# Sums in halves, scores of two chunks in a row, and a projection in one piece: a fused linear attention and MLP on one core

## The chip, the cores and the metric

The kernel runs on one core of one Trainium2 chip. The metric is the time of one execution in microseconds on the device; of several runs the median is given. Beside each time stands one profiled execution, whose span (first to last recorded instruction) is a little shorter than its own time. "The clock" is the granted TensorE clock, 1.00 being full speed.

Engines are called as in the profile: PE (matmuls), PEld (PE's weight loads), DVE, ACT, POOL, and SP, which issues most DMAs here.

## The reference: what is computed

Two parts follow each other, for 4 batches, 8 heads, 768 tokens and 64 elements a head:

```
state = gamma[h] * state + k[t]^T v[t]          # per batch and head, gamma = 1 - 2**(-5-h)
y[t]  = q[t] . state / sqrt(64)
x     = y, heads side by side                   # [4, 768, 512]
h     = (x^T U V)^T                             # U 768x32, V 32x768: over tokens
u     = x + h
out   = u + relu(u w1) w2                       # w1 512x2048, w2 2048x512
```

The kernel takes and gives float32 and computes the matmuls on bfloat16 operands.

## The kernel before

**A planner sets the order.** Nothing is issued when the code reaches it. Every step is given to a planner (class Plan, L65) by `add` with its cost by engine, the tiles it reads and writes, a due time and sometimes a hold (no earlier than). `run` (L116) then picks, again and again, the step with the earliest start, and of several the one that is due first; the steps of an engine are emitted in that order, and the tile framework adds the waits. So the costs, the due times and the planner's model of when a load lands (`load_cast`, L350, is one) and when an earlier result is ready (`ready`, L25) decide the order of all five engines' instruction queues. A change of the PE's array form between two steps is charged 0.093 us (`SWITCH`). Operations of POOL and DVE that are marked with a lock are not laid beside each other, and `behind` (L329) makes POOL's operation wait for the DVE operation in front of it where the planner has them within 3 us.

**Work.** The MLP of batch b carries the attention of batch b + 1 beside it, so that PE always has matmuls: startup with batch 0's attention, then MLP(0) beside attention(1), MLP(1) beside attention(2), MLP(2) beside attention(3), and MLP(3) alone (main loop, L1139 to L1169).

*Attention of batches 0 and 1* goes by pairs of heads, with PE transposes (`pair`, L480). *Attention of batches 2 and 3* goes by chunks of 128 tokens with all 8 heads (`loads_chunk` L653, `chunk` L662): three loads of 256 KB by SP; k cast by POOL or ACT, q and v scaled by the decay on POOL; k and q transposed by two DMAs on SP (L687, kT and qT, 4 and 4 buffers); the score (eight matmuls in 64x128 form, two of them side by side on the two halves of the rows, L692) into the PSUM tile RR[0], which is two banks (keys RR0, RR1); the mask product a = score x mask on DVE, 1024 elements (L700); the state's matmul into the PSUM tile Y and its eviction to ns; `mixes`, the matmuls with the earlier state and with a, into RR[1] (key RR2); and the eviction of that to x.

*The low rank part.* `proj` (L737) multiplies x by U into Y, 24 matmuls in 128x32 form, given to the planner as two steps (token blocks 0 to 3, 16 matmuls, then 4 and 5, 8 matmuls). `expand` (L753) multiplies by V into RR and adds x (L770, DVE, 512 elements per instruction): u, in the place of x. `turn_u` (L797, L798) transposes u by six DMAs on SP into uT, `turn_lo` (L774) does batch 1's low part on PE.

*The MLP* (`mlp`, L818) has 16 "lo" groups of four matmuls with 512 columns (tokens 0 to 511), then 8 "hi" groups with two times 256 columns; each group ends in a relu of 512 elements per partition (L836 ACT, or L838 DVE) into gT. The product with w2 then follows for r = 0, 1, 2 (two blocks of 128 tokens each), by seven products of 8 matmuls each of a Strassen-like scheme (`prod`, L930) into the PSUM tiles M0 to M2. They take as operands gT itself and sums of its quarters S1, S2, S4 and a difference left in gT, made on DVE (`sums`, L890, recorded at the helper's L302 as S and gT), as well as T1 to T4, sums over w2 (`w2_sums`, L1126, recorded as T and w2b). DVE evicts the products (L945, r5, r6 and halves of o), POOL prepares t12, t22 and t21 (L948, from ACT's copy s1 of the first product and from u), and the output is stored (L987).

`sums(part, m0, nm_, at)` gives four dependent DVE operations: S1 = A01 + A11, A01 = A00 - A01, S2 = S1 - A00, S4 = A10 - S2. Part 0 is tokens 0 to 511 (r = 0, 1), in four quarters of two m each, part 1 is the rest (r = 2), in two halves of four m each: 512 elements per instruction in all of them.

PSUM is full: RR0 to RR3, Y, M0 to M2 are its eight banks.

The lines that the profile puts operations to are often helpers': L305 is every matmul but the transposes (L309), L302 a two-operand operation on DVE or POOL, L297 a copy on ACT, L299 one on DVE or POOL, L342 a load on SP.

Of the kernel before, what the change touches and what calls it, by code (L numbers as in the profile page):

```python
# [18 lines left out]
class Step:  # L19
# [181 lines left out]
def kernel(  # L201
# [459 lines left out]

    def chunk(b, n, at):  # L662
        (kin, kk), (qin, qk), (vin, vk) = (gets.pop((nm, b, n)) for nm in "kqv")
        kd, kdk = new_kb()
# [21 lines left out]
        for src, dst, sk, dk in ((kd, kT, kdk, kTk), (qd, qT, qdk, qTk)):  # L686
# [13 lines left out]
        add({"D": cD(2 * DM)}, lambda e: nc.vector.tensor_tensor(  # L700
            a[:, :2 * DM].rearrange("p (n t) -> p n t", t=P),
            RR[0].rearrange("p i (n t) -> p (i n) t", t=P),
            mask[:, None, :].to_broadcast([P, H, P]), op=ALU.mult),
            ["RR0", "RR1", "mask"], zz(ak), at + 0.3)

# [7 lines left out]
        def mixes(e):  # L713
            if n:
                prev = ns[:, ds(4 * ((n - 1) % 5), 4)]
                for c in range(NC):
                    mm(RR[1][:, 0, ts(c, P)], qT[:, ts(c, P)], prev[:, c], start=(c == 0))
            for c in range(NC):
                for i in range(2):
                    h = 2 * c + i  # L720
                    mm(RR[1][:, 0, ts(h, D)], av[:, i, c], vd[:, ts(h, D)],
                       start=(n == 0 and h == 0))
# [9 lines left out]
        add({"PE": 0.24 + (0.23 if n else 0)}, mixes,  # L732
            [qTk, *nsk, *zz(ak), *zz(vdk)], ["RR2"], at + 1.9, F, slack=sl)
        evac(xs[b % 2][:, n], RR[1][:, 0], DM, ["RR2"], xk(b, [n], ALLC), at + 2.4)


    def proj(b, at):  # L737
        sl = 0.3

        def f(js):  # L740
            def g(e):
                for j in js:
                    for c in ALLC:
                        mm(Y[ds(RK * c, RK), :P], Ub[:, j], xs[b % 2][:, j, ts(c, P)],
                           start=(j == 0), stop=(j == NCK - 1))
            return g
        add({"PE": 0.25}, f(range(4)), xk(b, range(4), ALLC) + ["Ub"], ["Y"], at,
            ("cn", "cn"), slack=sl)
        add({"PE": 0.13}, f(range(4, 6)), xk(b, range(4, 6), ALLC) + ["Ub"], ["Y"],
            at + 0.1, ("cn", "cn"), slack=sl)  # L750
        evac(pcs, Y[:, :P], P, ["Y"], ["pcs"], at + 0.3)

    def expand(b, j0, nj, at):  # L753
        def f(e):
            for j in range(j0, j0 + nj):
                for c in ALLC:
                    mm(RR[c // 2][:, c % 2, ts(j - j0, P)], V4[ds(RK * c, RK), ts(j, P)],
                       pcs[ds(RK * c, RK)])
        keys = [f"RR{c}" for c in ALLC]
        add({"PE": 0.057 * nj + 0.02}, f, ["pcs", "V4"], keys, at, ("rn", "rn"),  # L760
            slack=0.2)
        x = xs[b % 2]
        for j in range(j0, j0 + nj, 2):
            for z in range(2):
                cc = (2 * z, 2 * z + 1)
                xj = x[:, ds(j, 2), ts(z, 256)].rearrange("p j (c f) -> p c j f", c=2)
                src = RR[z][:, :, ds((j - j0) * P, 256)].rearrange(
                    "p c (j f) -> p c j f", f=P)
                kk = xk(b, (j, j + 1), cc)
                add({"D": cD(512)}, lambda e, xj=xj, src=src: nc.vector.tensor_tensor(  # L770
                    xj, src, xj, op=ALU.add), [f"RR{c}" for c in cc] + kk,
                    kk + [("u", b % 2, i, z) for i in (j, j + 1)], at + 0.3)

# [40 lines left out]
    def next_m():  # L814
        mring[0] += 1
        return f"M{(mring[0] - 1) % 3}"

    def mlp(b, T, span, banks=()):  # L818
# [26 lines left out]
        for m in range(NM):  # L845
# [21 lines left out]
            relu(gT[:, m, :LO], bank, [bank], [("g", m, 0)], at + 0.9)  # L867
        yield
        for m in range(0, NM, 2):
# [13 lines left out]
            relu(gT[:, ds(m, 2), LO:], bank, [bank], [("g", m, 1), ("g", m + 1, 1)],  # L883
                 at + 0.9)
# [5 lines left out]
        def sums(part, m0, nm_, at):  # L890
# [3 lines left out]
            def A(z, w):  # L894
                return ge[:, z, w, ms, r]
            ek = [("g", 2 * m, part) for m in range(m0, m0 + nm_)]
            ok = [("g", 2 * m + 1, part) for m in range(m0, m0 + nm_)]

            def sk(n):
                return [(n, m, part) for m in range(m0, m0 + nm_)]  # L900
            for dst, a_, b_, op, rd, wr in (
                    (S1[:, ms, r], A(0, 1), A(1, 1), ALU.add, ek + ok, sk("S1")),
                    (A(0, 1), A(0, 0), A(0, 1), ALU.subtract, ek, ek),
                    (S2[:, ms, r], S1[:, ms, r], A(0, 0), ALU.subtract,
# [17 lines left out]
        for r in range(NB):  # L922
            part = 0 if r < 2 else 1
            ek = [("g", m, part) for m in range(0, NM, 2)]
            ok = [("g", m, part) for m in range(1, NM, 2)]

# [49 lines left out]
            at = prod(be, gl(0, 1), T3, ek + tk, False)  # L976
            dve(ob[:, HD:], be, tmp["r5"], ["r5"], [(obk, 1)], at)
# [148 lines left out]
    def w2_sums():  # L1126
        w2e = w2b.rearrange("p (m z) (h n) -> p z h m n", z=2, h=2)
        for j in range(4):
            ms = ds(2 * j, 2)
            B11, B21, B22, B12 = (w2e[:, 0, 0, ms], w2e[:, 1, 0, ms],  # L1130
                                  w2e[:, 1, 1, ms], w2e[:, 0, 1, ms])
            for dst, a_, b_ in ((T3[:, ms], B22, B12), (B12, B12, B11),
                                (T2[:, ms], B22, B12), (T4[:, ms], B21, T2[:, ms])):
                add({"D": 0.5}, lambda e, dst=dst, a_=a_, b_=b_:
                    both(e, dst, a_, b_, ALU.subtract), [("w2", j)], [("T", j)],
                    T[0] + 14 + j, lock="D")
# [76 lines left out]
```

## Time and profile before

| | us |
|---|---|
| median of 3 runs | 223.75 (223.63 to 224.15) |
| the profiled execution's own time | 224.59 |
| its span | 222.8 |
| PE busy in it | 211.8 |
| DVE, ACT, POOL busy | 143.9, 111.7, 87.0 |

How to read it: the profile's durations come from the one profiled execution, so a sum over them is held against 224.59, and its difference to the median is carried along. A group of instructions is given as: line, engine, operation, tile written <- tiles read, partitions x elements and type, count | busy time in all, mean ns of one | idle time of the engine ahead of them and what ended it. For a matmul the first pair of numbers is the form of the array that it uses. In a timeline several instructions of one group in a row are merged: the start of the first, the time from it to the end of the last, and the count; matmuls overlap in the pipeline, so the end of one lies behind the start of the next. The wait in brackets is the engine's idle time ahead of the instruction and whose result ended it.

### The profile page before, as it was taken

How to read it: one execution, taken by the hardware profiler on the slowest of the kernel's cores; microseconds unless marked ns; L12 is line 12 of the kernel's file. 1: busy time of each engine (PE TensorE's matmuls, PEld its weight loads, DVE VectorE, ACT ScalarE, POOL GpSimd, SP SyncE). 2: the span in 40 equal slices, each digit the busy share in tenths (PEclk: the TensorE clock that was granted, in tenths of full speed). 3: DMA queues.
4: the chain of work that ended last, by engine and by line, in shares of the span. 5: the costliest groups of instructions: out<-in, count | busy, mean ns of one | idle time of the engine just before them, and what ended most of it. 6: DMA issues, size and time to landing. Idle time of an engine off the chain costs nothing.

```text
span 222.8 us, 5876 instructions
## 1 busy us (share of the span) xinstructions
PE 211.8 (95%) x2391; PEld 152.4 (68%) x2405; DVE 143.9 (65%) x297; ACT 111.7 (50%) x214; POOL 87.0 (39%) x143
## 2 busy tenths in 40 slices
PE   7867999999999999999999999999999999999993
PEld 2556644488788885457887875458888854588882
DVE  4486717998897636798677856867858525345332
ACT  8856537679684335678621105686510036761000
POOL 4665900114768554311368453316134510003330
PEclk9999999999999999999999999999999999999998
DMA  5999999999599979897479989986105730000222
GB/s 167 301 291 224 157 195 206 233 289 297 140 222 212 154 205 182 218 170 142 96 158 190 222 195 202 195 187 123 26 0 143 181 106 3 0 0 3 94 97 94
DMA packets 85163, 35.22 MB, mean 158 GB/s; under 512 B 59920, under 2 KB 83216, under 8 KB 85136
## 3 DMA queue, kind: packets, MB, share of 16 engines
q1 hardware_dynamic: 78944, 25.93, 55.0%
q0 software_dynamic: 6192, 8.91, 19.3%
q8 instruction: 19, 0.31, 0.6%
q14 instruction: 8, 0.07, 0.1%
HBM read 27.75 MB, written 6.29 MB: 153 GB/s over the span
## 4 chain that ended last, share of the span: by engine, by line
PE 63%; DVE 16%; DMA 7%; POOL 5%; issue 4%; ACT 2%; SPq 1%; POOLq 0%; DVEq 0%
PE M L305 51%; PE RR L305 8%; DVE S L302 4%; DMA in<-in_v_dram 4%; DMA in<-in_k_dram 3%; PE Y L305 3%; DVE T L302 2%; POOL t L302 2%; DVE x L770 2%; ACT gT L836 1%; DVE gT L302 1%; SPq L342 1%; DVE o L945 1%; POOL out_dram L987 1%; DVE x L299 1%
## 5 line engine op out<-in xcount | busy, mean ns | idle before, releaser
L305 PE MATMUL M<-uT,w1b 128*128 128x256 bf16 (+1 forms) x489 | 85.7, 324 | 0.7 <-issue 0.3
L836 ACT ACTIVATE gT<-M 128x512 bf16<-128x512 f32 x88 | 51.9, 597 | 34.1 <-PE M L305 33.5
L305 PEld LDWEIGHTS <-w1b 128*128 128x128 bf16 x512 | 48.0, 98 | 29.6 <-issue 0.8
L305 PEld LDWEIGHTS <-gT 128*128 128x128 bf16 x409 | 39.3, 99 | 10.6 <-issue 3.7
L302 POOL TENSOR_TENSOR t<-s,x 128x256 f32<-128x256 f32 x36 | 23.1, 669 | 34.9 <-DVE S L302 21.8
L305 PEld LDWEIGHTS <-S 128*128 128x128 bf16 (+1 forms) x336 | 28.1, 97 | 4.4 <-issue 0.4
L305 PE MATMUL M<-w2b,gT 128*128 128x256 bf16 x192 | 26.7, 273 | 0.1
L305 PE MATMUL M<-w2b,S 128*128 128x256 bf16 x192 | 26.1, 273 | 0.3 <-DVE r L945 0.3
L305 PE MATMUL M<-T,gT 128*128 128x256 bf16 x192 | 25.1, 273 | 0.5 <-DVE r L945 0.4
L302 POOL TENSOR_TENSOR qb<-in,gqn 128x512 bf16<-128x512 f32 x12 | 12.5, 1044 | 27.9 <-DVE S L302 11.6
L302 DVE TENSOR_TENSOR S<-gT 128x512 bf16<-128x512 bf16 x24 | 11.6, 485 | 18.0 <-ACT gT L836 17.9
L945 DVE TENSOR_TENSOR r<-M,t 128x256 f32<-128x256 f32 x24 | 10.1, 421 | 12.6 <-POOL t L302 11.7
L297 ACT ACTIVATE s<-M 128x256 f32<-128x256 f32 x12 | 4.6, 385 | 26.7 <-PE M L305 26.7
L987 POOL DMA_DIRECT2D out_dram<-o x18 | 10.1, 563 | 19.3 <-DVE o L945 19.3
L770 DVE TENSOR_TENSOR x<-RR,x 128x512 bf16<-128x512 f32 x24 | 15.2, 683 | 2.1 <-PE RR L305 2.1
L297 ACT ACTIVATE kb<-in 128x512 bf16<-128x512 f32 (+1 forms) x18 | 10.0, 582 | 13.0 <-DMA in<-in_k_dram 12.9
L700 DVE TENSOR_TENSOR a<-RR,mask 128x1024 bf16<-128x1024 f32 x12 | 14.6, 1218 | 1.4 <-PE RR L305 1.2
L302 POOL TENSOR_TENSOR vb<-in,gkn 128x512 bf16<-128x512 f32 x12 | 12.5, 1045 | 6.8 <-DMA in<-in_v_dram 3.0
L945 DVE TENSOR_TENSOR o<-M,r 128x256 f32<-128x256 f32 x24 | 10.1, 423 | 6.4 <-PE M L305 6.1
L305 PE MATMUL M<-T,S 128*128 128x256 bf16 x96 | 12.6, 273 | 0.0
L297 ACT ACTIVATE ns<-Y 64x256 bf16<-64x256 f32 (+1 forms) x24 | 9.4, 392 | 5.4 <-PE Y L305 3.8
L302 DVE TENSOR_TENSOR gT<-gT 128x512 bf16<-128x512 bf16 x24 | 11.5, 481 | 0.6
(104 smaller groups left out, 258.4 us busy)
## 6 DMA issues: line engine op xcount, KB each, us to landing
out_dram<-o POOLq DMA_DIRECT2D x18, 256.0 KB, 3.5
in<-in_q_dram SPq DMA_DIRECT2D x8, 384.0 KB, 6.0
in<-in_k_dram SPq DMA_DIRECT2D x12, 256.0 KB, 5.0
in<-in_q_dram SPq DMA_DIRECT2D x12, 256.0 KB, 4.5
in<-in_v_dram SPq DMA_DIRECT2D x12, 256.0 KB, 4.7
in<-in_k_dram SPq DMA_DIRECT2D x7, 384.0 KB, 6.2
in<-in_v_dram SPq DMA_DIRECT2D x7, 384.0 KB, 6.3
w2b<-in_moe_w_ch_dram POOLq DMA_DIRECT2D x4, 512.0 KB, 15.2
```

The source lines that it names most:

```text
L297: nc.scalar.activation(dst, src, AF.Copy)
L299: (nc.vector if e == "D" else nc.gpsimd).tensor_copy(out=dst, in_=src)
L302: (nc.vector if e == "D" else nc.gpsimd).tensor_tensor(dst, a, b, op=op)
L305: nc.tensor.matmul(out_, lhsT, rhs, start=start, stop=stop, skip_group_check=True)
L342: nc.sync.dma_start(out=dst, in_=src)
L700: add({"D": cD(2 * DM)}, lambda e: nc.vector.tensor_tensor(a[:, :2 * DM].rearrange("p (n t) -> p n t", t=P), RR[0].rearrange("p i (n t) -> ...
L770: add({"D": cD(512)}, lambda e, xj=xj, src=src: nc.vector.tensor_tensor(xj, src, xj, op=ALU.add), [f"RR{c}" for c in cc] + kk, kk + [("u", ...
L836: nc.scalar.activation(dst, src, AF.Relu)
L945: add({"D": cD(HD)}, lambda e: nc.vector.tensor_tensor(dst, bankof(bank)[:, :HD], src, op=op), [bank] + rd, wr, at - 2)
L987: lambda e: (nc.sync if last else nc.gpsimd).dma_start(out=dst, in_=src), rd, [("out", b, at)], at,
```

## The change

1. `sums` for part 0 in two halves rather than four quarters, and for part 1 in one set of all eight m, issued inside r == 0 of the product loop behind POOL's t's (it also names "t21" as read, so that it is planned behind them). `w2_sums` in two rather than four. So each instruction has 1024 rather than 512 elements. New keys "h" let the difference left in gT be waited for on its own. The planner's cost of each is `cD(1024, 2)` rather than 0.5.
2. `chunks` gives the scores of two neighbouring chunks as one PE step, the even one into RR[0], the odd one into RR[1]; `mixes` of each goes into its own RR[z].
3. `proj` is one step of 24 matmuls.
4. In batches 2 and 3 the additions of `expand` are due 6 us later.
5. The planner's model: a DVE result is ready for DVE 0.03 us after its end; `load_cast` is charged less; the first loads of batch 0's pairs are given an order among themselves.

The tokens of q in pairs, of which the change's short description speaks, are in none of its lines. `PART1` is set and not used. The diff, cut to its core:

```diff
@@ ready
-            t = max(t, p.free if p.eng == e else p.end + Plan.LAG[p.eng] + s.slack)
+            t = max(t, p.free if p.eng == e != "D" else
+                    p.end + (0.03 if p.eng == e else Plan.LAG[p.eng] + s.slack))
@@ load_cast
-            dma=(nd, 0.009 + size / 27200 * 1.17, 0.9, 1.0), hold=hold)
+            dma=(nd, 0.0045 + size / 27200, 0.9, 1.0), hold=hold)
@@ load_pair
+        first = [] if b else ["in"]
-                 P * n, 512, [(key, i) for i in g], at + 0.01 * g[0], hold,
+                 P * n, 512, [(key, i) for i in g] + first, at + 0.01 * g[0], hold,
@@ chunk
+        z = n % 2
+        keys = [f"RR{2 * z}", f"RR{2 * z + 1}"]
-                    mm(RR[0][:, i, ts(c, P)], kT[r, ts(c, P)], qT[r, ts(c, P)])
-        add({"PE": 0.24}, score, [kTk, qTk], ["RR0", "RR1"], at, ("rw", "rw"),
-            slack=sl)
+                    mm(RR[z][:, i, ts(c, P)], kT[r, ts(c, P)], qT[r, ts(c, P)])
+        yield score, [kTk, qTk], keys
-            ["RR0", "RR1", "mask"], zz(ak), at + 0.3)
+            keys + ["mask"], zz(ak), at + 0.3 + z)
-            [qTk, *nsk, *zz(ak), *zz(vdk)], ["RR2"], at + 1.9, F, slack=sl)
-        evac(xs[b % 2][:, n], RR[1][:, 0], DM, ["RR2"], xk(b, [n], ALLC), at + 2.4)
+            [qTk, *nsk, *zz(ak), *zz(vdk)], keys[:1], at + 1.9, F, slack=sl)
+        evac(xs[b % 2][:, n], RR[z][:, 0], DM, keys[:1], xk(b, [n], ALLC), at + 2.4)
+    def chunks(b, n, at):
+        two = [chunk(b, n + z, at + DN * z) for z in range(2)]
+        told = [next(c) for c in two]
+        def scores(e):
+            for f, _, _ in told:
+                f(e)
+        add({"PE": 0.45}, scores, [k_ for t_ in told for k_ in t_[1]],
+            [k_ for t_ in told for k_ in t_[2]], at + DN, ("rw", "rw"), slack=0.4)
+        for c in two:
+            list(c)
@@ proj
-        add({"PE": 0.25}, f(range(4)), xk(b, range(4), ALLC) + ["Ub"], ["Y"], at,
+        add({"PE": 0.37}, f(ALLN), xk(b, ALLN, ALLC) + ["Ub"], ["Y"], at,
             ("cn", "cn"), slack=sl)
-        add({"PE": 0.13}, f(range(4, 6)), xk(b, range(4, 6), ALLC) + ["Ub"], ["Y"],
-            at + 0.1, ("cn", "cn"), slack=sl)
@@ expand
-                    kk + [("u", b % 2, i, z) for i in (j, j + 1)], at + 0.3)
+                    kk + [("u", b % 2, i, z) for i in (j, j + 1)],
+                    at + (6.3 if b > 1 else 0.3))
@@ sums
-                add({"D": 0.5}, lambda e, dst=dst, a_=a_, b_=b_, op=op:
+                add({"D": cD(nm_ * (256 if part == 0 else 128), 2)},
+                    lambda e, dst=dst, a_=a_, b_=b_, op=op:
-        for q4 in range(4):
-            sums(0, 2 * q4, 2, T + unit * (0.864 * 4 * (q4 + 1) + 1.0))
-        for q4 in range(2):
-            sums(1, 4 * q4, 4, T + unit * (13.8 + 0.872 * 4 * (q4 + 1) + 1.0))
+        for z in range(2):
+            sums(0, 4 * z, 4, T + unit * (0.864 * 8 * (z + 1) + 1.0))
@@ mlp, product loop, behind the three pool(...) of t12, t22, t21
+            if r == 0:
+                sums(1, 0, 8, at + 1)
@@ w2_sums
-        for j in range(4):
-            ms = ds(2 * j, 2)
+        for j in range(0, 4, 2):
+            ms = ds(2 * j, 4)
@@ main loop
-                chunk(b, n, base + 2 + 4.6 * n)
+                if n % 2:
+                    chunks(b, n - 1, base + 2 + 4.6 * (n - 1))
```

More of the change, by code (lines that the diff above doesn't have):

```diff
@@ L701, in chunk @@
             a[:, :2 * DM].rearrange("p (n t) -> p n t", t=P),
-            RR[0].rearrange("p i (n t) -> p (i n) t", t=P),
+            RR[z].rearrange("p i (n t) -> p (i n) t", t=P),
             mask[:, None, :].to_broadcast([P, H, P]), op=ALU.mult),
-            ["RR0", "RR1", "mask"], zz(ak), at + 0.3)
+            keys + ["mask"], zz(ak), at + 0.3 + z)
         def state(e):
@@ L716, in mixes @@
                 for c in range(NC):
-                    mm(RR[1][:, 0, ts(c, P)], qT[:, ts(c, P)], prev[:, c], start=(c == 0))
+                    mm(RR[z][:, 0, ts(c, P)], qT[:, ts(c, P)], prev[:, c], start=(c == 0))
             for c in range(NC):
@@ L720, in mixes @@
                     h = 2 * c + i
-                    mm(RR[1][:, 0, ts(h, D)], av[:, i, c], vd[:, ts(h, D)],
+                    mm(RR[z][:, 0, ts(h, D)], av[:, i, c], vd[:, ts(h, D)],
                        start=(n == 0 and h == 0))
@@ L816, in next_m @@
         return f"M{(mring[0] - 1) % 3}"
+    PART1, DN = 24.0, 2.0
     def mlp(b, T, span, banks=()):
@@ L866, in mlp @@
                         [bank], at + 0.4 * z, F)
-            relu(gT[:, m, :LO], bank, [bank], [("g", m, 0)], at + 0.9)
+            relu(gT[:, m, :LO], bank, [bank], [("g", m, 0), ("h", m, 0)], at + 0.9)
         yield
@@ L882, in mlp @@
                     [w1key(m)], [bank], at + 0.4 * z, F)
-            relu(gT[:, ds(m, 2), LO:], bank, [bank], [("g", m, 1), ("g", m + 1, 1)],
+            relu(gT[:, ds(m, 2), LO:], bank, [bank], [("g", m, 1), ("g", m + 1, 1), ("h", m, 1)],
                  at + 0.9)
@@ L896, in sums @@
             ek = [("g", 2 * m, part) for m in range(m0, m0 + nm_)]
+            hk = [("h", 2 * m, part) for m in range(m0, m0 + nm_)]
             ok = [("g", 2 * m + 1, part) for m in range(m0, m0 + nm_)]
@@ L901, in sums @@
             for dst, a_, b_, op, rd, wr in (
-                    (S1[:, ms, r], A(0, 1), A(1, 1), ALU.add, ek + ok, sk("S1")),
-                    (A(0, 1), A(0, 0), A(0, 1), ALU.subtract, ek, ek),
+                    (S1[:, ms, r], A(0, 1), A(1, 1), ALU.add,
+                     ek + hk + ok + ["t21"] * part, sk("S1")),
+                    (A(0, 1), A(0, 0), A(0, 1), ALU.subtract, ek, hk),
                     (S2[:, ms, r], S1[:, ms, r], A(0, 0), ALU.subtract,
@@ L924, in mlp @@
             ek = [("g", m, part) for m in range(0, NM, 2)]
+            hk = [("h", m, part) for m in range(0, NM, 2)]
             ok = [("g", m, part) for m in range(1, NM, 2)]
@@ L975, in mlp @@
             dve(tmp["r5"], de, tmp["t22"], ["t22"], ["r5"], at)
-            at = prod(be, gl(0, 1), T3, ek + tk, False)
+            at = prod(be, gl(0, 1), T3, hk + tk, False)
             dve(ob[:, HD:], be, tmp["r5"], ["r5"], [(obk, 1)], at)
@@ L1127, in w2_sums @@
         w2e = w2b.rearrange("p (m z) (h n) -> p z h m n", z=2, h=2)
-        for j in range(4):
-            ms = ds(2 * j, 2)
+        for j in range(0, 4, 2):
+            ms = ds(2 * j, 4)
+            wk, tk = [("w2", j), ("w2", j + 1)], [("T", j), ("T", j + 1)]
             B11, B21, B22, B12 = (w2e[:, 0, 0, ms], w2e[:, 1, 0, ms],
@@ L1133, in w2_sums @@
                                 (T2[:, ms], B22, B12), (T4[:, ms], B21, T2[:, ms])):
-                add({"D": 0.5}, lambda e, dst=dst, a_=a_, b_=b_:
-                    both(e, dst, a_, b_, ALU.subtract), [("w2", j)], [("T", j)],
+                add({"D": cD(1024, 2)}, lambda e, dst=dst, a_=a_, b_=b_:
+                    both(e, dst, a_, b_, ALU.subtract), wk, tk,
                     T[0] + 14 + j, lock="D")
```

## The prediction

> **What bounds the kernel now.** Read first the page (busy time per engine, the chain that ended last), then the same busy times by stage.
>
> ```profile
> span 222.8 us, 5876 instructions
> ...
> PE 211.8 (95%) x2391; PEld 152.4 (68%) x2405; DVE 143.9 (65%) x297; ACT 111.7 (50%) x214; POOL 87.0 (39%) x143
> ...
> PE 63%; DVE 16%; DMA 7%; POOL 5%; issue 4%; ACT 2%; SPq 1%; POOLq 0%; DVEq 0%
> ```
>
> ```profile
> 0.00:33.00 33.00, 27.22 (x423) 16.89 (x428) 18.19 (x47) 21.66 (x41) 18.93 (x42) 1.00 1.05 223
> 33.00:84.50 51.50, 50.70 (x698) 38.31 (x698) 39.57 (x79) 32.70 (x63) 22.27 (x40) 1.00 1.02 218
> 84.50:132.20 47.70, 47.22 (x503) 33.86 (x505) 35.60 (x68) 21.79 (x43) 21.84 (x28) 1.00 0.92 175
> 132.20:179.70 47.50, 47.21 (x480) 34.48 (x481) 32.78 (x62) 20.10 (x40) 17.11 (x23) 1.00 0.64 129
> 179.70:222.80 43.10, 39.42 (x297) 28.89 (x296) 17.74 (x44) 15.48 (x27) 6.86 (x11) 0.99 0.14 50
> ```
>
> The columns after the length are the busy times of PE, PEld, DVE, ACT and POOL, then the granted clock. The stages are startup, then the MLPs of batches 0, 1, 2 and 3, each but the last with the next batch's attention beside it. From 33.0 to 179.7 us PE idles 0.80, 0.48 and 0.29 us, at a full clock. DVE is the next engine, with 12 to 15 us to spare in every stage. So from 33 us on, time comes only from what PE itself executes, or from these few idle moments. The waits of PE from 33 us on, with total, times and longest:
>
> ```profile
> PE M L305 <- DVE r L945: 0.6, 3, 0.3
> PE RR L305 <- DVE uT L299: 0.2, 1, 0.2
> PE M L305 <- DVE o L945: 0.2, 1, 0.2
> PE M L305 <- issue: 0.2, 1, 0.2
> ```
>
> All of PE's waits together are 1.2 us. Matmul ends are modelled, so distances between starts are the better measure below; by them such a stall is up to twice what its row says, some 2.2 us in all.
>
> **The change, part by part.** The two instruction orders agree on all engines for the first 34 us, and PE issues 2405 matmuls in both: no form of matmul changes, only the order. The startup (33 us) and what follows the last matmul stay.
>
> *1. Pairs of scores, and the projection in one go.* A score runs in 64-row form and the projection in 32-column form, among 128x128 work. PE's timeline in MLP(1), start and duration:
>
> ```profile
> 106.00 1.91 PE L305 MATMUL M<-uT,w1b 128*128 128x256 bf16 x16
> 107.84 0.40 PE L305 MATMUL RR<-qT,kT 64*128 64x128 bf16 x8
> 108.17 0.61 PE L305 MATMUL M<-uT,w1b 128*128 128x256 bf16 x4
> 108.84 1.91 PE L305 MATMUL M<-uT,w1b 128*128 128x256 bf16 x16
> 110.59 0.39 PE L305 MATMUL RR<-ns,qT 128*128 128x128 bf16 x4
> 111.92 1.04 PE L305 MATMUL M<-w2b,gT 128*128 128x256 bf16 x8
> 112.89 0.40 PE L305 MATMUL RR<-qT,kT 64*128 64x128 bf16 x8
> 113.22 1.05 PE L305 MATMUL M<-T,S 128*128 128x256 bf16 x8
> 114.10 1.04 PE L305 MATMUL M<-w2b,S 128*128 128x256 bf16 x8
> ...
> 117.27 0.41 PE L305 MATMUL Y<-x,Ub 128*32 128x128 bf16 x16
> 117.61 1.05 PE L305 MATMUL M<-T,gT 128*128 128x256 bf16 x8
> 118.59 0.29 PE L305 MATMUL Y<-x,Ub 128*32 128x128 bf16 x8
> 118.82 1.05 PE L305 MATMUL M<-w2b,S 128*128 128x256 bf16 x8
> ```
>
> Take starts. Sixteen matmuls ahead of a score last 106.00 to 107.84 = 1.84, ahead of full-size work 108.84 to 110.59 = 1.75: entering the 64-row form costs 0.09. Eight matmuls say the same: 111.92 to 112.89 = 0.97 against 113.22 to 114.10 = 0.88. A score lasts 0.33 from its start to the next work (107.84 to 108.17). Two scores in a row enter and leave that form once in place of twice; the exit taken at the price of the entry (a choice: its row shows only the 0.33 with the matmuls in it), a pair saves 0.2. Six pairs (batches 2 and 3, six chunks each): 1.2 us. The projection's sixteen last 0.34 and its eight 0.23, that is 0.12 once and 0.11 per eight; all 24 in a row should last 0.45 in place of 0.57, and one entry goes (117.61 to 118.59 = 0.98 against 0.88, 0.10): 0.22 a batch, 0.4 for two. Together 12 + 4 changes of form at 0.10 each: **−1.6**. It can't be hidden, since PE is solid in 84.5 to 179.7; lower end 0, if all of it turned into waits; upper end 1.6.
>
> *2. What the pair costs.* Both scores now wait for both chunks' transposed q and k. Tightest is batch 2's pair of chunks 4 and 5. Chunk 5's q is scaled on POOL, transposed by a DMA, and landed 3.5 us after issue; its score stood at 112.89 above:
>
> ```profile
> 105.94 1.04 POOL L302 TENSOR_TENSOR qb<-in,gqn 128x512 bf16<-128x512 f32 x1 [4.45 <-DVE S L302]
> ```
>
> ```profile
> L687 SPq DMA_TRANSPOSE qT<-qb x1: 1190/1190/1190, 107.0 to 107.0; - x1
> ...
> DMA to landing us min/median/max: 3.5/3.5/3.5
> ```
>
> So it landed at 107.0 + 3.5 = 110.5. In the new order PE reaches the pair at about 109.5. POOL's 4.45 us of waiting is for sums. Their last eight of 0.43 become four of 0.69 (item 3): 0.6 sooner; and a mask product of 1.22, that now stands between them, moves with its pair and may or may not stand there: the landing comes between 108.7 and 109.9. Bounds: 0 and 110.5 − 109.5 = 1.0; I take **+0.2**, since the estimate of the landing lies just ahead of need. The other five pairs stand 3 us and more behind their landings in the order.
>
> *3. Sums of 1024 elements.* The DVE's groups, mean ns behind the busy time:
>
> ```profile
> L770 DVE TENSOR_TENSOR x<-RR,x 128x512 bf16<-128x512 f32 x24 | 15.2, 683 | 2.1 <-PE RR L305 2.1
> L700 DVE TENSOR_TENSOR a<-RR,mask 128x1024 bf16<-128x1024 f32 x12 | 14.6, 1218 | 1.4 <-PE RR L305 1.2
> ...
> L302 DVE TENSOR_TENSOR S<-S,gT 128x512 bf16<-128x512 bf16 x24 | 10.2, 427 | 0.0
> ```
>
> 512 elements more cost 1218 − 683 = 535 ns with a PSUM operand, so 683 holds some 0.15 of fixed cost; a bf16 sum of 427 holds 0.15 + 0.27, and 1024 elements cost some 0.15 + 0.54 = 0.69 in place of 0.85. Bounds: 0.85 (nothing saved) and, at the other form's rate, 1.22. Ninety-six sums of this kind and 16 on w2 become 48 and 8: 56 x 0.16 = 9 us less DVE. It lies beside PE, so it is worth only the waits that it ends: I take the 0.80 of 33 to 84.5 as gone (the `DVE r` waits, where DVE is at 77%): **−0.8**, bounds 0 and −0.8, and of the wait `DVE uT` at the start of MLP(1) (0.2 by its row, up to twice that), half: **−0.2**, since one of these evictions passes from ACT to DVE.
>
> The Trainium skill, VectorE: DVE Perf Modes, section The TRN2 errata, gives a VectorE operation between SBUF tiles 58 cycles of fixed cost, 0.06 us at its 0.96 GHz; by that, an estimate, the 56 operations save 3.4 us and not 9, which would leave perhaps half of the waits and give 223.0. The 0.15 of the rows above speaks for the larger saving; no row here has a 1024-element bf16 sum.
>
> *4. Part 1's sums behind POOL's t's of r = 0.* They no longer stand ahead of t12. In the last batch this was a stall:
>
> ```profile
> 204.40 1.03 PE L305 MATMUL M<-T,gT 128*128 128x256 bf16 x8 [0.18 <-DVE r L945]
> ```
>
> That goes, but four sums of 0.69 then stand among the evictions of the products, which PE wants every 0.87 us: 0.2 to 0.3 late once. Even, **0**, bounds ±0.3. In MLP(1) the next step's t12 waits for the fourth of these sums on DVE: r6 comes up to 0.45 late there, while the 0.2 to 0.35 of `DVE o` (behind a mask product that moves away) goes: **+0.1**, bounds −0.35 and +0.45.
>
> *5. The planner believes in earlier loads and in DVE readiness 0.03 us after the end.* That is what reorders ACT. In the order after, the casts of batch 1's first k and q and kT (kb0 ahead of the first hi relu of MLP(0)) pass in among the eight hi relus. ACT now, and the first k's issue:
>
> ```profile
> 45.02 0.60 ACT L836 ACTIVATE gT<-M 128x512 bf16<-128x512 f32 x1 [0.27 <-PE M L305]
> ...
> 49.88 0.93 ACT L297 ACTIVATE kb<-in 128x384 bf16<-128x384 f32 x2
> ```
>
> ```profile
> L342 SPq DMA_DIRECT2D in<-in_k_dram x1: 384/384/384, 40.4 to 40.4; - x1
> ...
> DMA to landing us min/median/max: 6.2/6.2/6.2
> ```
>
> The load lands at 40.4 + 6.2 = 46.6. ACT has finished a relu at 45.6 and then waits 1.0 for it, with all hi relus queued behind. Then ACT has 8 relus (0.5 to 0.6), four pairs of casts (0.93) and one kT (0.8): 4.2 + 3.7 + 0.8 = 8.7 us in a stage in which PE needs 7.0. Late by 1.0 + 1.7 = 2.7; PE has two further M banks, 2 x 0.87 = 1.7 ahead: a stall of **+1.0**, bounds 0 (the casts fall behind the relus' slack) and 2.7 (no bank ahead).
>
> *6. u's additions later (batches 2, 3).* They follow the product's evictions. The third pair of additions, and the transposes that read them:
>
> ```profile
> 125.05 1.28 DVE L770 TENSOR_TENSOR x<-RR,x 128x512 bf16<-128x512 f32 x2
> ```
>
> ```profile
> 123.29 8.21 SPq L798 DMA_TRANSPOSE uT<-x  x6
> ```
>
> Each transpose takes SP 8.21 / 6 = 1.37, so the third pair is read from 128.8, and was ready at 126.3: 2.5 us of cover. The first pair keeps its place in the order. **0**; with the cover gone, each us later is a us for PE, which uses uT from 133.70:
>
> ```profile
> 133.70 0.59 PE L305 MATMUL M<-uT,w1b 128*128 128x512 bf16 x2
> ```
>
> *Sum.* −1.6 + 0.2 − 0.8 − 0.2 + 0 + 0.1 + 1.0 + 0 = −1.3. The profiled execution took 224.59 us (span 222.8 and 1.8 around it); it becomes 223.3, span 221.5. It ran 0.84 above the median of the runs, 223.75, so the median becomes 224.59 − 1.3 − 0.84 = 222.45, say **222.5**.
>
> **The rivals.** A difference under 0.2% (0.45 us) is about what a measurement of this kernel can tell from no change.
>
> *Stalls go as well.* If k lands a little sooner, or the planner's casts find ACT ahead, item 5 costs 0.2 and item 2 nothing: −1.3 − 0.8 − 0.2 = −2.3, **221.4**. For it: DVE has 9 us less to do. Against it: 46.6 is in the trace, and load issues ahead of it stay.
>
> *Nothing left.* The pair waits its full 1.0 for chunk 5's q, in place of 0.2, and item 4 costs its +0.3 and +0.45 rather than 0 and +0.1: −1.3 + 0.8 + 0.3 + 0.35 = +0.15, **223.9**. For it: PE's 95% leaves no slack to give a wait back. Or the sums save nothing (0.85 each): items 3's −1.0 goes, −0.3, **223.4**.
>
> *Slower: ACT's casts ahead of MLP(0)'s hi relus.* One queue, in order: relus wait behind a cast that waits for a load. Without banks ahead it costs 2.7, and 0.4 of the 0.8 stays as the later relus delay batch 0's sums: −1.3 + 1.7 + 0.4 = +0.8, **224.5**. It decides once the stalls that are new exceed the switches' 1.6 plus 0.45. For it: the load's time in the trace; against: two banks ahead, and DVE takes a relu now and then.
>
> *Longer sums hold POOL.* The `DVE S` in POOL's row above shows POOL waiting for sums; if each of POOL's t's waits 0.69 rather than 0.43 for one sum, that is 0.26 x 12 steps of r = 3.1 at most, less the cover of PE's 0.87 us per product: at full price −1.3 + 3.1 = +1.8, **225.5**. Against it: the sum of sums is shorter. The Trainium skill, SBUF — State Buffer, section SBUF: two separate sides, says a DVE operation with two SBUF inputs and a POOL operation that reads SBUF exclude each other for the whole instruction; by that rule this rival's mechanism exists, and the row of 105.94 agrees without proving it, as its wait can be a semaphore's.
>
> *It doesn't do what it says.* Tokens of q in pairs are in no line of the diff; nothing is costed for them.
>
> **How the numbers follow.** Forecast 222.5: 0.40. Stalls go as well, 221.4: 0.22. Nothing left, 223.4 to 223.9: 0.14. ACT's casts, 224.5: 0.18. POOL held, 225.5: 0.06. Faster by over 0.2%: 0.40 + 0.22 = 0.62; within: 0.14; slower: 0.24. The range reaches from 221.0 (below 221.4 by the part of the 2.2 us of stalls that may go besides) to 224.5; outside it lie POOL's case, half of ACT's and a small part of the second: 0.06 + 0.09 + 0.05 = 0.2. Faster cases hold most of it, 221.0 to 223.0.
>
> **What would show it.** Right: in 84.5 to 165 us scores come as x16, the projection x24, and PE's busy time there falls with the same matmuls; DVE's total is some 9 us less, with 1024-element sums at 0.69; ACT shows a cast waiting for a load at 45.6 and PE a stall of about 1 us before 52; no stall at 57 to 64, none at 204. Wrong: sums at 0.85 or 1.22 (item 3), a PE wait for a transposed q ahead of a pair at 109 (item 2), a uT wait at 133 or 180 (item 6), a stall over 2 us ahead of 52 (the slower rival).

## The result and the profile after

The changed kernel takes 222.6 us (median of 12 runs, 221.97 to 224.36) against 223.78 (12 runs, 223.25 to 224.47): ratio 0.9951, 95% interval 0.9929 to 0.9973. A second set, on another chip, gave 0.9920 (0.9892 to 0.9948). It is faster by 0.5 to 0.8%; 222.5 was forecast. Its profiled execution took 223.26 us, with a span of 221.4.

The page of the changed kernel, busy time by engine:

```profile
span 221.4 us, 5838 instructions
...
PE 209.2 (95%) x2391; PEld 151.6 (68%) x2405; DVE 134.2 (61%) x243; ACT 111.2 (50%) x210; POOL 91.6 (41%) x145
```

The same windows as before, first the length, then PE, PEld, DVE, ACT, POOL and the clock:

```profile
33.00:84.50 51.50, 49.67 (x689) 37.01 (x690) 37.52 (x61) 30.66 (x60) 26.66 (x41) 1.00 1.00 219
84.50:132.20 47.70, 47.51 (x510) 34.86 (x511) 33.30 (x57) 22.55 (x43) 20.66 (x28) 1.00 0.80 170
132.20:179.70 47.50, 47.29 (x485) 34.93 (x487) 29.95 (x49) 20.52 (x40) 19.02 (x26) 1.00 0.67 133
```

DVE is 143.9 − 134.2 = 9.7 us lighter. PE's idle time is 0.19 and 0.21 us in the second and third stage, where it was 0.48 and 0.29; but in the first it has grown from 0.80 to 1.83 us. What PE waited for, from 33 us on (total, times, longest):

```profile
PE Y L310 <- ACT kb L298: 1.4, 1, 1.4
PE M L306 <- ACT gT L854: 0.2, 1, 0.2
```

None of the four rows of before is left, and one long wait is new. PE's timeline and ACT's in MLP(0) show it:

```profile
41.23 5.82 PE L306 MATMUL M<-uT,w1b 128*128 128x512 bf16 x37
48.42 0.51 PE L310 MATMUL Y<-ident,kb 128*128 128x128 bf16 x6 [1.37 <-ACT kb L298]
...
51.40 1.91 PE L306 MATMUL M<-uT,w1b 128*128 128x256 bf16 x16 [0.24 <-ACT gT L854]
```

```profile
44.46 0.60 ACT L854 ACTIVATE gT<-M 128x512 bf16<-128x512 f32 x1 [0.27 <-PE M L306]
47.43 0.94 ACT L298 ACTIVATE kb<-in 128x384 bf16<-128x384 f32 x2 [2.37 <-DMA in<-in_k_dram]
```

ACT stands idle for 2.37 us with a cast whose load has not landed; PE stands behind it, since the transposes of that kb are next in its own queue, in the middle of the hi groups.

The changes of form are as forecast. Rows of PE's timeline in MLP(1):

```profile
108.43 1.91 PE L306 MATMUL M<-uT,w1b 128*128 128x256 bf16 x16
110.27 0.62 PE L306 MATMUL RR<-qT,kT 64*128 64x128 bf16 x16
110.82 1.05 PE L306 MATMUL M<-uT,w1b 128*128 128x256 bf16 x8
...
117.95 0.52 PE L306 MATMUL Y<-x,Ub 128*32 128x128 bf16 x24
118.41 1.05 PE L306 MATMUL M<-w2b,S 128*128 128x256 bf16 x8
```

Two scores last 0.55 from their start to the next work, where one lasted 0.33; the projection's 24 matmuls last 0.46, where 0.45 was forecast. There is no wait ahead of 110.27.

**Where the 1.46 us went.** PE's last matmul starts at 217.67 us in place of 219.13. The first matmul of MLP(0) on uT started 0.55 earlier, in a startup whose queues are identical in both kernels; that belongs to the two executions. The 16 changes of form are 1.55. By distances between starts, the stalls behind 33 us were 2.24 and are 2.82 (1.54 + 0.14 at 48, 0.40 at 51.4, 0.28 at 34, 0.17 at 85, 0.19 at 123.6, 0.10 at 206): 0.6 back. Together −1.5.

### The profile page after: what moved, and what is told of

It reads as the page before. It is cut to its first block, busy times and chain, and to the rows that moved or that the text cites. A ratio compares the mean times of both kernels' runs of the same rounds, so it can differ in the third digit from the quotient of the medians.

```text
span 221.4 us, 5838 instructions
## 1 busy us (share of the span) xinstructions
PE 209.2 (95%) x2391; PEld 151.6 (68%) x2405; DVE 134.2 (61%) x243; ACT 111.2 (50%) x210; POOL 91.6 (41%) x145
## 4 chain that ended last, share of the span: by engine, by line
PE 75%; DMA 15%; SPq 4%; POOL 2%; ACT 2%; issue 1%; DVE 0%; DVEq 0%; ACTq 0%; POOLq 0%
PE M L306 63%; PE RR L306 7%; DMA w2b<-in_moe_w_ch_dram 7%; DMA in<-in_k_dram 6%; SPq L343 4%; PE Y L306 3%; DMA T<-in_moe_U_dram 2%; POOL w1b L353 1%; ACT gT L854 1%; PE RR L310 1%; PE Y L310 1%; ACT kb L298 0%; POOL kb L303 0%; ACT qb L298 0%; DVE o L965 0%
## 5 line engine op out<-in xcount | busy, mean ns | idle before, releaser
L854 ACT ACTIVATE gT<-M 128x512 bf16<-128x512 f32 x84 | 49.9, 598 | 35.8 <-PE M L306 35.4
L306 PEld LDWEIGHTS <-S 128*128 128x128 bf16 (+1 forms) x336 | 28.1, 97 | 3.8
L306 PE MATMUL M<-w2b,S 128*128 128x256 bf16 x192 | 26.7, 273 | 0.0
L306 PE MATMUL M<-w2b,gT 128*128 128x256 bf16 x192 | 26.2, 273 | 0.0
L705 DVE TENSOR_TENSOR a<-RR,mask 128x1024 bf16<-128x1024 f32 x12 | 14.1, 1219 | 6.7 <-PE RR L306 6.7
L303 POOL TENSOR_TENSOR vb<-in,gkn 128x512 bf16<-128x512 f32 x12 | 13.0, 1080 | 11.5 <-DMA in<-in_v_dram 7.2
L298 ACT ACTIVATE x<-RR 128x512 bf16<-128x512 f32 (+2 forms) x19 | 11.5, 608 | 9.8 <-PE RR L306 9.6
L303 DVE TENSOR_TENSOR S<-gT 128x1024 bf16<-128x1024 bf16 x12 | 8.8, 730 | 11.9 <-ACT gT L854 11.7
L569 DVE TENSOR_TENSOR a<-RR,mask 128x1024 bf16<-128x1024 f32 (+1 forms) x12 | 11.0, 952 | 2.8 <-PE RR L306 2.6
L462 POOL CAST in<-w2b 1x1 f32<-1x1 bf16 x12 | 5.4, 482 | 17.2 <-DMA w2b<-in_moe_w_ch_dram 16.3
```

Of the source, the lines that this page charges most:

```text
L298: nc.scalar.activation(dst, src, AF.Copy)
L303: (nc.vector if e == "D" else nc.gpsimd).tensor_tensor(dst, a, b, op=op)
L306: nc.tensor.matmul(out_, lhsT, rhs, start=start, stop=stop, skip_group_check=True)
L462: add({"P": 0.18}, lambda e: nc.gpsimd.tensor_copy(out=t[:1, :1], in_=src), [rd], [(key, z) for z in range(2)], at)
L569: lambda e, bs=bs, lo=lo, w=w: nc.vector.tensor_tensor(av[:, :, ds(bs[0], len(bs))], RR[lo // 2][:, :, :w].rearrange("p i (b t) -> p i b t ...
L705: add({"D": cD(2 * DM)}, lambda e: nc.vector.tensor_tensor(a[:, :2 * DM].rearrange("p (n t) -> p n t", t=P), RR[z].rearrange("p i (n t) -> ...
```

## The experiments

Ratios are to the kernel before, on the same chip. The theory: the fewer changes of form and the fewer, longer sums pay, and the planner's new load model takes part of it back in MLP(0). The general rival: each part pays for itself, whatever stands beside it.

**The load model, undone in the changed kernel.** Of the whole change only this line is put back:

```diff
-            dma=(nd, 0.0045 + size / 27200, 0.9, 1.0), hold=hold)
+            dma=(nd, 0.009 + size / 27200 * 1.17, 0.9, 1.0), hold=hold)
```

> The changed kernel with one line of the planner's model put back: load_cast is charged as before, so that batch 1's first k casts and transposes stand behind all hi groups of MLP(0) again. Theory (the new model orders PE's transposes of kb0 ahead of their load, and that cost 1.5 + 0.4 + 0.1 us of PE between 47 and 52 us): the stall goes, median 2.0 under the changed kernel's 222.6, 220.6, ratio to before 0.986. Rival 1 (the stall goes, but the waits that the kernel before had between 57 and 64 us, 0.9 in all, return with the old place of the casts): 221.5, ratio 0.990. Rival 2 (the load is late wherever it stands, PE waits for it elsewhere): 222.6, ratio 0.995.

Measured: 222.29 us, ratio 0.9904 (0.9868 to 0.994). The transposes stand behind all hi groups again, and PE doesn't wait for kb:

```profile
45.81 5.95 PE L306 MATMUL M<-uT,w1b 128*128 128x256 bf16 x53
51.60 0.50 PE L310 MATMUL Y<-ident,kb 128*128 128x128 bf16 x6
```

The ratio is the one that rival 1 named, but its mechanism isn't there: the waits at 57 to 64 us did not return. The theory's 0.986 lies just outside the interval; the gain is smaller than 2.0, and the later runs show that the wait differs between executions.

**The load model alone, in the kernel before.** The same line, the other way round.

> The kernel before with that one line alone changed, and nothing else. Theory: PE waits for batch 1's first k between 46 and 52 us, about 1.5 to 2.0 in all; of the 0.9 us of waits between 57 and 64 us some goes; 224.9, ratio 1.005. Rival (casts and transposes earlier are worth as much as they cost): 223.8, ratio 1.000.

Measured: 224.24 us, 1.0002 (0.9969 to 1.0035): no loss. In its trace PE came late to the transposes, held up by 0.54 us at 41.9 (for an addition of DVE), and the load had landed at 46.4 rather than 47.3. The stalls at 57 to 64 and at 133 us are not in this trace either, though nothing but the load model was changed. So the wait is not a constant; the next two runs ask how it comes about.

**The changed kernel again, and beside it the one with the old load model.**

> The changed kernel itself, beside the three that follow. Its first runs gave 0.9951 [0.9929, 0.9973] of the kernel before. Theory (the wait for batch 1's first k in MLP(0) depends on when that load's gate opens, at 40 to 41.3 us, and so differs between executions by up to 1.5 us): 0.993 to 0.997, a PE wait for ACT's kb of 0 to 1.5 us around 47 us, and executions that differ by more than those of the kernel with the old load model. Rival (the wait is always 1.5): executions agree within 0.5 us.

> The first experiment's kernel again, now beside the changed kernel on the same chip: 0.9904 [0.9868, 0.994] of the kernel before then. Theory (no PE wait in MLP(0)): 1.0 to 1.5 us under the changed kernel, ratio to before 0.990. Rival (that result was the chip's): the same as the changed kernel, 0.995.

Measured: 222.63 us, 0.9920 (0.9892 to 0.9948), and 221.23 us, 0.9872 (0.9837 to 0.9907). So the old line is worth 1.4 us beside the rest of the change (1.0 by the ratios of the first runs); its runs lie between 220.96 and 222.1, those of the changed kernel between 221.74 and 223.09, which is not clearly wider. In the executions with the transposes early, PE starts them 1.07 us behind the load's landing (ACT's cast lies between), or when it gets there, 19.7 us behind its first matmul on uT, whichever is later. (In the first three rows the record of that first matmul is missing: its weights are loaded 0.22 us before the start shown.)

| execution | first matmul on uT | load landed | PE gets there | transposes start | stall |
|---|---|---|---|---|---|
| changed kernel | 27.39 | 47.34 | 46.88 | 48.42 | 1.54 |
| again | 27.06 | 46.83 | 46.54 | 47.90 | 1.36 |
| with single scores (below) | 26.72 | 46.29 | 46.21 | 47.36 | 1.15 |
| with u due as before (below) | 27.93 | 45.77 | 47.66 | 47.66 | 0 |

Four more executions of other kernels here have the transposes early, and the same rule gives their starts within 0.05 us: a stall of 0.1 in one with the old `ready`, none in the other, none with the sums of 512, and none with the load model alone (where the 0.54 at 41.9 comes on top of the 19.7).

The last row in PE's and ACT's timelines of that kernel, with the cast at once behind its relu and no idle time on either engine:

```profile
42.00 5.82 PE L306 MATMUL M<-uT,w1b 128*128 128x512 bf16 x38
47.66 0.50 PE L310 MATMUL Y<-ident,kb 128*128 128x128 bf16 x6
```

```profile
45.24 0.60 ACT L853 ACTIVATE gT<-M 128x512 bf16<-128x512 f32 x1 [0.27 <-PE M L306]
45.85 0.94 ACT L298 ACTIVATE kb<-in 128x384 bf16<-128x384 f32 x2
```

**Pairs of scores and the projection in one piece, alone in the kernel before.** `chunks` and the 24-matmul `proj` are taken over as the diff has them, and nothing else.

> The kernel before with the scores in pairs and the projection in one piece, and nothing else: 16 changes of the array's form fewer (99 for 115). Theory (0.097 us each, on a PE that is never idle there): -1.55, 222.2, ratio 0.993. Rival (the pair waits for the second chunk's transposed q and gives half back): 223.0, ratio 0.9965, with a PE wait for DMA qT ahead of a score of 16 matmuls.

Measured: 224.42 us, 0.9994 (0.9961 to 1.0027). Nothing is gained; by the median that is less than even the rival gave, whose 0.9965 the interval just holds. The 16 changes are gone, and new waits stand in PE's timeline:

```profile
115.97 1.03 PE L305 MATMUL M<-T,gT 128*128 128x256 bf16 x8 [0.58 <-DVE r L960]
...
162.34 0.40 PE L305 MATMUL RR<-qT,kT 64*128 64x128 bf16 x8 [0.49 <-DMA qT<-qb]
```

By distances between starts they are 0.75, 0.65 and, at 177, 0.25, with 0.09 at 173: 1.74 against the 1.55 gained. The second is the wait for the second chunk's transposed q; the first comes from POOL, whose t12 stood behind a scaling of q that itself waited (in the kernel before, that scaling came after the t's, at 116.06):

```profile
113.79 1.04 POOL L302 TENSOR_TENSOR qb<-in,gqn 128x512 bf16<-128x512 f32 x1 [6.20 <-DMA in<-in_v_dram]
114.79 1.92 POOL L302 TENSOR_TENSOR t<-s,x 128x256 f32<-128x256 f32 x3
```

**Single scores in the changed kernel.** The other side of it: `chunk` and its call are as before, all else is changed.

> The changed kernel with one score at a time, as before, so that there are 111 changes of the array's form in place of 99. Theory (0.097 us each, and with the shorter sums the pair has no wait of its own, unlike the pairs-alone kernel, which gave 1.7 back): 12 x 0.097 = 1.2 over the changed kernel, ratio to before 1.000. Rival (the pair only trades changes of form for waits): 0.995.

Measured: 223.79 us, 0.9968 (0.994 to 0.9996), 1.16 over the changed kernel on the same chip (222.63). 12 x 0.097 = 1.16; that the two agree to the digit is chance, since each interval is 0.6 us wide to either side. Its trace has the stalls of the changed kernel (1.15 + 0.14 at 47, 0.40 at 50.3) and, from 36 us on, 0.17 at 84 and 0.15 at 115. From the first matmul on uT to the last matmul it is 1.0 us longer than the trace of the changed kernel's run beside it, with 0.3 less of stalls: 1.3. So a pair is worth its two changes of form, if nothing holds it.

**Sums of 1024 alone, in the kernel before.** `sums` and `w2_sums` as in the diff, part 1 behind POOL's t's.

> The kernel before with the sums of 1024 elements alone (halves of part 0, part 1 as one set behind POOL's t's of r = 0, sums on w2 in two). Theory (9 to 10 us less DVE, which ends PE's waits for evictions between 57 and 64, at 133 and at 204 us, 1.5 in all): 222.4, ratio 0.994. Rival (DVE was not what PE waited for, as its busy share of 65% says): 223.7, ratio 1.000.

Measured: 225.42 us, 1.0047 (1.0016 to 1.0078): slower, which neither expected. The waits at 57 to 64 us are gone, but PE stalls 0.51 + 0.17 at 85, 0.61 at 121 and 0.76 at 207.7. With 0.28 at 35 and 0.19 at 133 that is 2.5, only 0.3 over the kernel before; the rest of the 1.1 us between the medians isn't placed, and the interval reaches down to 0.4 us. The last stall, in DVE's and PE's timelines:

```profile
205.54 0.42 DVE L949 TENSOR_TENSOR o<-M,r 128x256 f32<-128x256 f32 x1
205.88 0.68 DVE L302 TENSOR_TENSOR S<-S,gT 128x1024 bf16<-128x1024 bf16 x1
206.59 0.69 DVE L302 TENSOR_TENSOR S<-gT,S 128x1024 bf16<-128x1024 bf16 x1
207.20 0.42 DVE L949 TENSOR_TENSOR o<-M,x 128x256 f32<-128x256 f32 x1
```

```profile
207.67 1.03 PE L305 MATMUL M<-w2b,gT 128*128 128x256 bf16 x8 [0.60 <-DVE o L949]
```

Two dependent sums, 1.3 us, stand between two evictions that PE wants every 0.87 us. The old `ready` lets the planner take a DVE result as ready when DVE is free, so a dependent sum counts as ready at the same moment as an eviction and wins by its due time. That makes a theory of its own: the sums pay only with the new `ready`.

**The sums with the new `ready`, in the kernel before.** The edit on top of the last one:

```diff
-            t = max(t, p.free if p.eng == e else p.end + Plan.LAG[p.eng] + s.slack)
+            t = max(t, p.free if p.eng == e != "D" else
+                    p.end + (0.03 if p.eng == e else Plan.LAG[p.eng] + s.slack))
```

> The kernel before with the sums of 1024 elements and the new `ready`, and nothing else. The sums alone were 1.0047 [1.0016, 1.0078]. Theory (the sums only pay with an order of DVE in which evictions come between two dependent sums): the wait at 207.7 goes (0.76) and the one at 121 shrinks (0.6), and what is left is the gain of 9 to 10 us of DVE at 57 to 64 and 133: 0.996 to 0.998. Rival (sums of 1024 cost whatever the order): 1.004.

Measured: 223.28 us, 0.9971 (0.9941 to 1.0002), 0.76% below the sums alone, as the theory gave; against the kernel before, the interval still touches 1. Its stalls behind 36 us are 0.38 at 84 and four of under 0.1. No run has the new `ready` alone, so what it is worth without the longer sums isn't shown.

**The changed kernel with the old `ready`, twice.**

> The changed kernel with the planner's `ready` as before, so that two dependent sums are planned back to back on DVE and evictions come behind two of them. Theory (a dependent sum of 1024 elements holds an eviction that PE waits for; in the sums-alone kernel such waits were 0.6 at 121 us and 0.76 at 207.7): a wait of PE for DVE o of 0.6 to 0.8 around 206 us comes back, 0.7 to 1.3 over the changed kernel, ratio to before 0.998 to 1.001. Rival (the order of DVE inside a product is not what PE waits for): 0.995.

> The changed kernel with the old `ready` once more. It lost 4.2 us to the changed kernel, of which its trace shows 3.6 as waits of PE behind 33 us (0.65 at 66, 2.2 between 165.6 and 168.5, 0.75 at 209.6), less about 1.2 that PE waits less for batch 1's first k, and 2.3 as a startup that ended later (29.4 against 27.1 us), though the first 33 us of all queues are the same. Theory (the startup was that one execution's): startup ends at 27 to 28, the waits stay, ratio to before 1.003 to 1.011. Rival (the startup is late in this kernel for a reason of its own): it ends at 29 again.

Measured: 226.80 us, 1.0101 (1.0066 to 1.0137), and 226.62, 1.0108 (1.0065 to 1.0151). Slower by 4 us than the changed kernel, far over the 0.7 to 1.3 that the theory gave: it placed one wait, and there are several. PE's and DVE's timelines in MLP(2), second run:

```profile
165.28 0.38 PE L305 MATMUL RR<-ns,qT 128*128 128x128 bf16 x4
165.50 0.40 PE L305 MATMUL RR<-vb,a 128*128 128x64 bf16 x8
166.42 0.38 PE L305 MATMUL RR<-ns,qT 128*128 128x128 bf16 x4 [0.52 <-DVE a L704]
166.64 0.40 PE L305 MATMUL RR<-vb,a 128*128 128x64 bf16 x8
168.07 1.03 PE L305 MATMUL M<-w2b,gT 128*128 128x256 bf16 x8 [1.04 <-DVE o L964]
```

```profile
162.35 0.42 DVE L964 TENSOR_TENSOR o<-M,r 128x256 f32<-128x256 f32 x1 [0.79 <-PE M L305]
162.69 0.68 DVE L302 TENSOR_TENSOR S<-gT 128x1024 bf16<-128x1024 bf16 x1
163.41 0.69 DVE L302 TENSOR_TENSOR gT<-gT 128x1024 bf16<-128x1024 bf16 x1
164.01 2.35 DVE L704 TENSOR_TENSOR a<-RR,mask 128x1024 bf16<-128x1024 f32 x2
166.28 0.68 DVE L302 TENSOR_TENSOR S<-S,gT 128x1024 bf16<-128x1024 bf16 x1
167.00 0.69 DVE L302 TENSOR_TENSOR S<-gT,S 128x1024 bf16<-128x1024 bf16 x1
167.60 0.42 DVE L964 TENSOR_TENSOR o<-M,x 128x256 f32<-128x256 f32 x1
```

Four sums, with both mask products of the pair among them, run between two evictions: 0.30 + 0.68 + 1.21 = 2.2 us of stall. With 1.04 at 65, 0.30 at 119 and 0.75 at 209 that is 4.3 in this execution (3.6 in the first). In the changed kernel the same sums have evictions among them, and the mask products stand ahead of them all:

```profile
162.63 0.68 DVE L303 TENSOR_TENSOR S<-gT 128x1024 bf16<-128x1024 bf16 x1
163.23 0.42 DVE L965 TENSOR_TENSOR o<-M,r 128x256 f32<-128x256 f32 x1
163.57 0.68 DVE L303 TENSOR_TENSOR gT<-gT 128x1024 bf16<-128x1024 bf16 x1
164.16 0.69 DVE L303 TENSOR_TENSOR S<-S,gT 128x1024 bf16<-128x1024 bf16 x1
164.77 0.42 DVE L965 TENSOR_TENSOR o<-M,x 128x256 f32<-128x256 f32 x1
```

With the old `ready` the startup ended at 29.4 and at 28.5 us, later than in the other profiled executions (26.7 to 28.1); why is open. So the 4 us are not all DVE's order. Against the first execution of the changed kernel, PE's last matmul starts 4.1 and 3.7 us later; 2.0 and 1.4 of that are the later startup (1.4 by the first weights loaded for uT). The rest is less than the stalls of 3.6 and 4.3, since kb's wait, 2.08 there, is 0.65 and 0 here.

**Sums of 512 in the changed kernel.** `sums` and `w2_sums` as before, all else changed.

> The changed kernel with sums of 512 elements, in quarters, part 1's in front of the product as before. Theory (9 to 10 us more on DVE; the pairs then wait, as in the pairs-alone kernel, where PE waited 0.75 behind a late t12 at 116 and 0.65 for a transposed q at 162, and the waits at 57 to 64 and 204 return): 1.2 to 2.2 over the changed kernel, 0.998 to 1.002 of the kernel before. Rival (the sums bring nothing beside the new `ready`): 0.992.

Part 1's sums are back ahead of the product with it. Measured: 224.63 us, 1.0029 (1.0 to 1.0058), 1.1% over the changed kernel's 0.992, about 2.4 us and just above what the theory gave. The places differ from the named ones: 0.75 at 57, 0.45 + 0.52 + 0.51 at 84 to 86, 0.45 at 115.7 (for r, as in the kernel with the pairs alone), and 0.18 at 176. No pair waits for its q, and the stall at 204 did not return. So beside the rest of the change, the 1024-element sums with part 1's new place are worth more than the whole of the change.

**u's additions due as before, in the changed kernel.** Only `at + 0.3` in `expand` is put back.

> The changed kernel with u's additions due as before; only DVE's order differs (in batches 2 and 3 two additions of 0.68 stand ahead of r5 or o of the product instead of behind). My forecast priced this part at 0. Theory (an eviction 0.68 to 1.28 late leaves PE waiting for a bank of M, which it wants every 0.87): PE waits of 0.3 to 0.8 at about 122 and 168 us, 0.5 to 1.2 over the changed kernel. Rival (forecast): no difference, 0.992 of the kernel before.

Measured: 222.55 us, 0.9915 (0.9888 to 0.9943), the same as the changed kernel's 0.9920. The forecast's 0 holds, my theory of 0.5 to 1.2 falls: PE's rows show no wait at 122 or 168 us. By distances between starts it loses 0.20 at 122.4, but the changed kernel loses the same at 123.6 (0.19).

## Why the prediction was right, and where it was wrong

The time was right, in part by luck. Two groups of its terms were off, on opposite sides: the planner's model (5) cost 2.08 where 1.0 was forecast, and the waits of items 2 and 4, priced at +0.3 together, came out at −0.4. By the parts, the profiled execution should have gained 1.0; its startup, which no part touches, gave 0.55 more.

*1, the changes of form (−1.6): right.* The single scores in the changed kernel cost 1.16 by the medians for 12 changes, 0.097 each, and 1.3 by the traces; the projection's four were only read from rows (0.46 for 24 matmuls).

*2, the pair's wait (+0.2): 0 in both executions of the changed kernel.* The mechanism is real: alone in the kernel before, the pair waited 0.65 for a transposed q, at another pair than the one named (batch 3's, at 162), and POOL's t12 behind the pair's q cost 0.75 more. The changed kernel has neither. With the sums of 512 (and part 1's old place) t12 stands behind a scaling of q again and PE loses 0.45 at 115.7, so the 1024-element sums spare it that wait; what spares it the wait for q is not shown. That one isn't gone for good: in the second execution with the old load model a pair waits 0.2 by its row for its q, at 135.5.

*3, the sums (−1.0): size right, reason incomplete.* 0.69 was forecast; the groups of the changed kernel's DVE (mean ns behind the busy time) show 0.68 to 0.75:

```profile
L303 DVE TENSOR_TENSOR S<-S,gT 128x1024 bf16<-128x1024 bf16 x12 | 9.0, 754 | 0.0
L303 DVE TENSOR_TENSOR S<-gT 128x1024 bf16<-128x1024 bf16 x12 | 8.8, 730 | 11.9 <-ACT gT L854 11.7
L303 DVE TENSOR_TENSOR gT<-gT 128x1024 bf16<-128x1024 bf16 x12 | 8.3, 691 | 0.2
L303 DVE TENSOR_TENSOR S<-gT,S 128x1024 bf16<-128x1024 bf16 x12 | 8.2, 684 | 0.1
```

The waits of 57 to 64 us went, all of the 0.8, and of the 0.4 at 85 there is 0.17 left, as forecast. But the sums are not their only remedy, since the load model alone ends them too; and that less DVE work ends PE's waits is false by itself: the sums alone cost 0.47%. The estimate of 3.4 us saved, from the fixed cost of 58 cycles in a table of the Trainium skill (VectorE: DVE Perf Modes, The TRN2 errata), is under the measured one: 43.5 us in the four groups of before, 34.3 in these, 9.2 saved; the text under that table says itself that its VectorE row predicts too little and that the measured fixed term is about 150 cycles, 0.16 us by its 0.96 GHz, an estimate. The 0.15 of the rows agrees.

*4, part 1's place (0 and +0.1): −0.24 and −0.16.* The stall at 204 (0.34) went, and 0.10 at 206 came. The one at 133 (0.35) went, and in MLP(1) the wait that was named is there: t12 waits for the fourth sum, r6 comes late, and PE loses 0.19 at 123.6. POOL's row:

```profile
122.21 1.92 POOL L303 TENSOR_TENSOR t<-s,x 128x256 f32<-128x256 f32 x3 [0.74 <-DVE S L303]
```

That the new place ended the two stalls is not shown: the one at 133 is gone with the load model alone as well, and the one at 204 is gone with the sums of 512 in their old place. No run has part 1's place alone.

*5, the planner's model (+1.0): the step that failed, twice.* First, its size and way: the wait was 2.08 in the profiled execution (1.54 + 0.14 + 0.40), since PE's own queue had the transposes of kb among the hi groups, and the two M banks that I counted as cover don't matter to an engine that waits at its own next instruction. Only the 0.40 came over the banks. The casts moved by the load model alone. The 2.08 is one execution's: in the others with this order it lies between 0 and 1.9. Second, `ready` was priced at nothing of its own ("that is what reorders ACT" is said of both); it reorders DVE. With the old `ready` the changed kernel is 4 us slower, 1% slower than before; PE's stalls for DVE are 3.6 and 4.3 us of its two traces, and its late startup stays open.

*6, u's additions (0): right*, by the run that put them back.

Of the rivals, the one that ended slower named the right place and the right load, and its price of 2.7 was nearer to the profiled execution than my 1.0; its sign, a stall over 2 us ahead of 52, was there with 2.08. It didn't decide, since the stalls at 57 to 64 went all the same, and those at 133 and 204, of which the forecast had counted none as net gain.

The kernel with the old load model beats both: 221.23 us, ratio 0.9872, and 0.9904 in its first runs.

## What to carry to other kernels

A part's worth depends on its company, so the general rival falls: the pairs are worth 0 alone and 1.2 us beside the rest of the change; the 1024-element sums cost 1 us alone (at least 0.4) and save over 2 beside the pairs and a readiness rule that lets evictions between them. When operations on a shared engine get longer, look at what stands between the short ones that the busiest engine waits for. And if an order is planned ahead, an optimistic load time isn't free: list what it moves into the in-order queue of the busiest engine, not only into that of the engine that casts.

## What the runs showed of the hardware

A sum that starts while POOL computes is stretched by about what POOL has left. In the sums-alone kernel, DVE and POOL at 117 us:

```profile
117.31 1.45 DVE L302 TENSOR_TENSOR S<-gT 128x1024 bf16<-128x1024 bf16 x1
118.79 0.69 DVE L302 TENSOR_TENSOR gT<-gT 128x1024 bf16<-128x1024 bf16 x1
```

```profile
117.17 1.04 POOL L302 TENSOR_TENSOR vb<-in,gkn 128x512 bf16<-128x512 f32 x1
```

The first sum takes 1.45 us, the next of its size, with POOL idle, 0.69. The Trainium skill, SBUF — State Buffer, section SBUF: two separate sides, says that a DVE operation with two SBUF inputs and a POOL operation that reads SBUF exclude each other for the whole instruction; this pair of rows agrees, in the direction of POOL holding DVE. So do all fourteen traces: 68 sums start with more than 0.15 us of a POOL operation of two inputs still to run, and each takes its own 0.43 or 0.69 plus what is left of that operation, less 0.13 to 0.15. The other direction shows as well: eleven scalings on POOL start with over 0.3 us of a running sum left, and take 1.22 to 1.50 in place of 1.04, again what is left less 0.14. The startup, with identical queues for 33 us, ended between 26.7 and 28.1 us in twelve profiled executions of ten kernels (the two with the old `ready` aside), and in them the first k's load landed between 45.4 and 47.3: where a planned order comes within a microsecond of a load's landing, one execution waits and the next does not.
